# One core, one long list: the same 2118 entries handed to the scheduler in another order

## The chip, the core and the metric

The kernel runs on one core of a Trainium2 chip. The metric is the device time of one execution in microseconds (us); lower is better. The core has five engines that each work through their own instructions in program order: PE (TensorE, matmuls), DVE (VectorE), ACT (ScalarE), POOL (GpSimd) and SP (SyncE, which here only issues DMAs). They meet at semaphores: an instruction that needs another engine's result waits at the head of its own engine's queue, and everything behind it on that engine waits too.

## The reference: what is computed

There are two parts. The first is attention with a local window: 4 batches of 8 heads, 768 positions, 64 columns a head. Each position sees the positions less than 16 away, and 24 summaries of 32 positions each (the maximum of the keys, the mean of the values). The second is a network on the attention's result `x` (3072 rows of 512): `h = x @ w_in`, `g = h * cos(h)`, `out = g @ w_out`, with 2048 columns in the middle.

```python
mask_l = np.abs(pos[:, None] - pos[None, :]) < window
scores_s = scale * np.einsum('bhsd,bhnd->bhsn', q, k_sum) + np.log(block)
scores_all = np.concatenate([np.where(mask_l, scores_l, -1e9), scores_s], axis=-1)
a = np.exp(scores_all - np.max(scores_all, axis=-1, keepdims=True))
a = a / (np.sum(a, axis=-1, keepdims=True) + 1e-09)
x = np.matmul(a, np.concatenate([v, v_sum], axis=2))      # then heads side by side
h = x @ w_in
out = (h * np.cos(h)) @ w_out
```

## The kernel before

**Blocks, groups and steps.** The 3072 rows are cut into 8 blocks of 384 (two to a batch). In each block the attention of two heads is one *group*: a, b, c and d, so `c4` is the third group of block 4. The network of one block is 16 *steps*, one for each 128 of the 2048 middle columns. Steps are numbered through, s0 to s127: s0 to s5 do columns 0 to 5 of block 0 (their sums are put away), s6 to s21 all of block 1, s22 to s31 the rest of block 0, and from s32 on each block has 16 in a row. A step needs the `x` of all four groups of its block, in two parts (high and low). In its first product the groups are used in the order a, b, c, d, three matmuls each.

**Weights.** Each of the 16 weight slices w0 to w15 comes as 64-bit numbers and is turned by ACT, DVE (three passes of bit work) and POOL into a high and a low part. This is done once, between 11 and about 152 us, and works partly in PSUM banks and in the two "stage" tiles.

**The list.** The whole program is one list of entries, `ORDER`, read by the loop at the end. Each entry is `who.what.arguments`. The order of the entries of one engine is the order in which that engine runs them. Where two entries share a buffer, the one listed later waits for the one listed earlier. Numbers in `up`, `sc`, `ms`, `tq`, `tk`, `tp`, `va`, `dh` and `sh` are PSUM banks (there are 8); a last letter a, v or p is the engine (ACT, DVE, POOL).

The entries of a group, by engine: on SP `q`, `k`, `v`, `m` (loads; `m` takes the value summaries, from line 485), `po` and `pi` (out to DRAM and back, lines 640 and 647). On PE `tq` and `tk` (transposes), `ms` (the mask as a matmul), `sc` (scores, line 561), `tp` (transpose of the weights of the attention, line 618), `va` (values, line 662). On DVE `ks`, `mx` (maximum, line 580), `sm` (sum, line 601), `iv` (reciprocal, line 606), `qt`, `kt`, `pt` (transposes in squares of 32, lines 512, 517, 632) and `xl` (low part of x, line 348). On POOL `su` (less the maximum, line 585) and `nm` (normalize, line 609). On ACT `ex` (exp, line 598). `z` (line 572), `cp`, `cq`, `ck` and `xh` (line 342 on ACT, 344 on DVE) move results out of PSUM on the engine that their letter names.

So one group is a chain over all engines: `sc`, `z`, `mx`, `su`, `ex`, `sm`, `iv`, `nm`, then `tp` and `cp` (or, from group c2 on, `pt`, `po`, `pi`), `va`, `xh`, `xl`.

The entries of a step: `up` (PE, line 706: 12 matmuls into one bank), `tu` (ACT, line 716), `re` (DVE, line 719), `si` (ACT, line 724), `ga` (DVE, line 728; the bank is free after it), `hi` (ACT line 342 or DVE line 344), `lo` (DVE or POOL, line 348), `dh` and `dl` (PE, line 757: 6 and 3 matmuls into three banks of sums). `re` and `ga` of one step lie on DVE with `si` on ACT between them. After the last step of a block, `ta` and `st` take the sums out and store them.

A weight slice has `l` (load), `ab`, `cl`, `sh`, `lb`, `fb`, `hi`, `lo`; the value summaries `v0_1` and so on have `l`, `h` and `s`.

**Buffers that couple the engines.** The three tiles of a step (`t`, `gh`, `gl`) have two buffers each: a third `tu` waits for an earlier step's `lo`, a third `hi` for an earlier `dh`, a third `lo` for an earlier `dl`. The tile of loaded keys (`kn`) and that of loaded queries (`qn`) have one buffer from block 2 on.

## Time and profile before

| | us |
|---|---|
| median of 3 runs | 661.62 |
| lowest and highest of them | 660.22 and 662.21 |
| profiled execution, its own time | 663.55 |
| span in that execution, first to last instruction | 661.8 |
| PE busy | 633.2 |
| DVE busy | 449.9 |
| ACT busy | 305.8 |
| POOL busy | 220.7 |

The profile comes from one execution. A span is the time from the first to the last instruction. A group row gives the line, the engine and operation, output and inputs, the tile shapes, a count, the busy time, the mean ns of one, and the idle time of that engine before these instructions with what ended it.

### The profile page before, as it was taken

The page shows a single profiled execution, that of the slowest core. Times are in us where ns is not written, and L with a number is a line of the kernel's source. Part 1 is how long each engine was busy: PE and PEld are TensorE (multiplying, and loading weights), DVE is VectorE, ACT ScalarE, POOL GpSimd, SP SyncE. Part 2 cuts the span into 40 slices and gives each one's busy share as a digit, 9 for nine tenths or more (in the row PEclk, how much of TensorE's full clock was granted, in tenths as well). Part 3 has the DMA queues.
Part 4 walks back from the last instruction along what each step waited for, and adds up shares of the span by engine and source line. Part 5 has one row for each costly group of instructions (what it writes and reads, how often), then busy time and mean ns, then how long its engine had stood idle before and what let it go on. Part 6 is the DMA issues. An engine that isn't in the chain of part 4 may idle for free.

```text
span 661.8 us, 13155 instructions
## 1 busy us (share of the span) xinstructions
PE 633.2 (96%) x5141; PEld 560.9 (85%) x5141; DVE 449.9 (68%) x798; ACT 305.8 (46%) x512; POOL 220.7 (33%) x219
## 2 busy tenths in 40 slices
PE   6378999999999999999999999999999999999996
...
GB/s 222 257 271 188 289 16 215 173 113 63 59 125 82 93 120 122 139 58 113 109 104 137 137 96 106 116 43 85 108 169 101 93 94 76 0 1 17 16 17 48
DMA packets 167158, 72.67 MB, mean 110 GB/s; under 512 B 136825, under 2 KB 155833, under 8 KB 167097
## 3 DMA queue, kind: packets, MB, share of 16 engines
...
q8 instruction: 40, 0.66, 0.4%
...
## 4 chain that ended last, share of the span: by engine, by line
PE 86%; DMA 4%; SPq 3%; DVE 3%; POOL 2%; ACT 1%; issue 1%; DVEq 0%; POOLq 0%; ACTq 0%
PE banks L757 39%; PE banks L706 39%; PE banks L561 4%; PE banks L662 3%; DMA late<-in_moe_w_out_dram 2%; SPq L448 2%; DMA late<-in_moe_w_in_dram 1%; DMA late<-in_q_dram 1%; DVE banks L391 1%; DVE stage L407 1%; POOL stage L385 1%; ACT stage L380 1%; SPq L477 0%; PE banks L548 0%; DVE banks L399 0%
## 5 line engine op out<-in xcount | busy, mean ns | idle before, releaser
L706 PE MATMUL banks<-xh,w 128*128 128x384 f32 x1024 | 272.1, 337 | 0.2 <-ACT pt L342 0.2
L757 PE MATMUL banks<-w,gh 128*128 128x512 f32 x768 | 198.1, 393 | 0.0
L706 PEld LDWEIGHTS banks<-xh,w 128*128 128x128 f32 x1024 | 185.9, 188 | 2.9 <-ACT pt L342 0.4
L706 PE MATMUL banks<-xl,w 128*128 128x384 f32 x512 | 171.4, 335 | 0.0
L757 PEld LDWEIGHTS banks<-w,gh 128*128 128x128 f32 x768 | 142.6, 188 | 28.8 <-ACT gh L342 0.3
L716 ACT ACTIVATE t<-banks 128x384 int32<-128x384 f32 x128 | 62.5, 489 | 164.8 <-DVE gl L348 60.2
L348 POOL TENSOR_TENSOR gl<-t,gh 128x384 fp32r<-128x384 f32 x55 | 56.4, 1026 | 224.0 <-PE banks L757 108.3
L719 DVE SCALAR_TENSOR_TENSOR t<-t,banks 128x384 f32<-128x384 int32 x128 | 69.9, 548 | 67.3 <-ACT t L716 66.4
L757 PE MATMUL banks<-w,gl 128*128 128x512 f32 x384 | 109.8, 394 | 1.0 <-DVE gl L348 1.0
L724 ACT ACTIVATE t<-t 128x384 f32<-128x384 f32 x128 | 66.5, 524 | 75.5 <-DVE t L719 75.1
L706 PEld LDWEIGHTS banks<-xl,w 128*128 128x128 f32 x512 | 96.1, 188 | 1.6
L757 PEld LDWEIGHTS banks<-w,gl 128*128 128x128 f32 x384 | 71.1, 188 | 15.5 <-DVE gl L348 1.1
L585 POOL TENSOR_TENSOR sc<-sc,m 128x720 f32<-128x720 f32 x28 | 40.1, 1431 | 130.3 <-DVE m L580 130.3
L728 DVE TENSOR_TENSOR t<-t,banks 128x384 f32<-128x384 f32 x128 | 69.1, 544 | 13.4 <-ACT t L724 12.4
L609 POOL TENSOR_TENSOR sc<-sc,r 128x720 f32<-128x720 f32 x28 | 39.9, 1426 | 48.9 <-DVE r L606 45.6
L342 ACT CAST gh<-t 128x384 fp32r<-128x384 f32 x68 | 34.7, 511 | 43.9 <-DVE t L728 22.4
L348 DVE TENSOR_TENSOR gl<-t,gh 128x384 fp32r<-128x384 f32 x73 | 41.5, 569 | 18.0 <-PE banks L757 9.8
L344 DVE CAST gh<-t 128x384 fp32r<-128x384 f32 x60 | 23.1, 384 | 28.6 <-PE banks L757 26.8
L348 POOL TENSOR_TENSOR w<-stage,w 128x1024 fp32r<-128x1024 f32 x15 | 36.3, 2418 | 10.4 <-ACT w L342 8.5
L572 DVE SCALAR_TENSOR_TENSOR sc<-banks,mask 128x360 f32<-128x360 f32 x48 | 24.4, 524 | 21.2 <-PE banks L561 21.2
L561 PEld LDWEIGHTS banks<-kd,qd 64*64 64x64 f32 x1344 | 28.4, 135 | 9.2 <-issue 6.6
L662 PEld LDWEIGHTS banks<-pt,vn 120*64 120x64 f32 x624 | 21.0, 141 | 13.0 <-ACT pt L342 7.0
(101 smaller groups left out, 602.1 us busy)
## 6 DMA issues: line engine op xcount, KB each, us to landing
...
```

Of the source, the lines that this page charges most:

```text
L342: eng.copy(out=out, in_=in_)
L348: eng.tensor_tensor(out=lo, in0=src, in1=hi.bitcast(F32), op=ALU.subtract)
L561: nc.tensor.matmul(out=self.sp[hh][s * QT : (s + 1) * QT, c, lo : lo + n], lhsT=self.qd[rows, t * QT : (t + 1) * QT], rhs=self.kd[rows, ke ...
L585: nc.gpsimd.tensor_tensor(out=self.sc, in0=self.sc, in1=self.m.unsqueeze(2).broadcast_to([P, U, NK]), op=ALU.subtract)
L609: nc.gpsimd.tensor_tensor(out=self.sc, in0=self.sc, in1=self.r.unsqueeze(2).broadcast_to([P, U, NK]), op=ALU.mult)
L662: nc.tensor.matmul(out=self.xps[rows, t * QT : (t + 1) * QT], lhsT=self.vn[:, t, rows], rhs=self.pt[2 * c + hh][s], start=True, stop=True,)
L706: nc.tensor.matmul(out=self.h, lhsT=w_of(name, self.f)[:, c * P : (c + 1) * P], rhs=x_of(self.blk, part, c), start=n == 0, stop=n == last,)
L716: nc.scalar.activation(out=self.t.bitcast(I32), in_=self.h, func=AF.Copy, scale=1.0 / TWO_PI, bias=0.25)
L719: nc.vector.scalar_tensor_tensor(out=self.t, in0=self.t.bitcast(I32), scalar=-TWO_PI, in1=self.h, op0=ALU.mult, op1=ALU.add)
L724: nc.scalar.activation(out=self.t, in_=self.t, func=AF.Sin, scale=-1.0, bias=-0.5 * math.pi)
L728: nc.vector.tensor_tensor(out=self.t, in0=self.t, in1=self.h, op=ALU.mult)
L757: nc.tensor.matmul(out=self.acc[i], lhsT=g[:, i * P : (i + 1) * P], rhs=w_of(name, self.f), start=self.first and n == 0, stop=self.last an ...
```

## The change

`ORDER` is replaced by another list of the same 2118 entries: each entry of the old list is in the new one, on the same engine. What differs is the order on each engine and the PSUM banks in the arguments, which follow the order. No function, shape or buffer count changes. The diff is cut to the beginning, the end, and the places that the prediction speaks of.

```diff
--- before.py
+++ after.py
@@ -25,147 +25,147 @@
...
-b0.k a0.q a0.k c0.q c0.k b0.tk.0.0 d0.k b0.ks.0 a0.tq.1 b0.tk.1.2 v0_1.l b0.ks.1 a0.tk.0.3 a0.cq.v v0_0.l a0.tk.1.4
-b0.ck.0.v a0.ck.0.a a0.ks.0 a0.ms.5.6 a0.ck.1.a a0.ks.1 b0.q a0.sc c0.tk.0.7 a0.z.1.a a0.z.0.v w1.l c0.ck.0.a a0.mx
-d0.tk.0.1 c0.ks.0 a0.su c0.tq.0 c0.tk.1.3 d0.q c0.cq.a d0.tk.1.4 c0.ms.6.5 d0.ks.1 a0.ex v0_1.h.p c0.ks.1 c0.ck.1.v
-w0.l d0.ks.0 c0.sc a0.sm c0.v c0.z.1.a v0_0.h.v b0.tq.7 c0.z.0.a b0.ms.0.3 b0.ck.1.a a0.iv v0_0.s.p b0.cq.a v0_1.s.v
-d0.ck.0.a b0.sc w1.ab.0 c0.mx c0.m d0.tq.5 b0.z.1.a w1.cl.v c0.su d0.ms.2.1 b0.z.0.a w2.l w1.sh.6.7 d0.cq.a d0.ck.1.a
-d0.sc w1.lb a0.nm c0.ex a0.v d0.z.1.a w1.fb.1 a0.tp.0.3 d0.z.0.a a0.tp.1.0 w0.ab.0 a0.m d0.mx w1.hi.a w0.cl.v d0.su
-d0.m c0.sm w0.sh.4.5 w5.l w1.lo.p c0.iv w2.ab.0 w0.lb c1.m a0.cp.0.a w2.cl.v c0.nm d0.ex b1.q w0.fb.1 a0.cp.1.a w3.l
-a0.va.1 d0.sm w0.hi.a d1.m w2.sh.6.7 w0.lo.p c0.tp.0.2 c1.q d0.iv w5.ab.0 w2.lb b1.tq.3 a1.q a0.xh.a d0.nm c0.tp.1.0
-w2.fb.1 c0.cp.0.a d0.v c0.cp.1.a w5.cl.v w2.hi.a c0.va.2 a0.xl w2.lo.p d0.tp.0.6 c0.xh.a w5.sh.4.5 w4.l d0.tp.1.7 a1.m
-b0.mx w3.ab.0 a1.tq.0 w5.lb b0.su a1.v a1.cq.a a1.ms.1.0 w5.fb.1 w3.cl.p b0.ex b0.m d0.cp.0.a a1.sc b0.sm b1.cq.a
-c1.tq.6 d0.cp.1.a c0.xl a1.z.1.a d0.va.3 b0.iv w3.sh.4.5 b0.nm a1.z.0.a b1.m c1.ms.7.2 d0.xh.a a1.mx c1.cq.a d1.q
-w4.ab.0 c1.sc w3.lb a1.su b0.v b0.tp.0.0 w5.hi.a b0.tp.1.1 d0.xl w4.cl.v c1.z.0.a c1.v b0.cp.0.a w4.sh.6.7 c1.z.1.a
-b1.ms.3.0 b0.cp.1.a v1_0.l c1.mx a1.ex w8.l w4.lb c1.su b0.va.2 b1.sc a1.sm b0.xh.a w5.lo.p c1.ex d1.tq.1 b0.xl
-b1.z.1.a a2.q a1.iv s0.up.2 w4.fb.0 b1.z.0.a a1.nm w3.fb.1 w4.hi.a a1.tp.0.0 d1.cq.a w4.lo.v w9.l d1.ms.3.6 s0.tu
-a1.cp.0.a b1.v c1.sm w8.ab.0 a1.tp.1.7 d1.sc s0.re c1.iv a1.cp.1.a s1.up.4 w8.cl.v c1.nm w10.l s0.si b1.mx d1.v
-w8.sh.0.1 w3.hi.a b1.su a1.va.5 d1.z.0.v s1.tu c1.tp.0.7 w8.lb w3.lo.p a2.v d1.z.1.a c1.tp.1.3 a2.tq.6 s1.re c1.cp.1.a
-a1.xh.a s2.up.3 d1.mx s1.si c1.cp.0.a s0.ga d1.su w7.l w8.fb.0 s0.hi.a c1.va.2 s0.lo.p w9.ab.1 s1.ga w6.l s3.up.7
-w8.hi.v s2.tu b2.q s1.hi.v d1.ex w9.cl.v s1.lo.p a1.xl s0.dh.0.1.4 s2.re w8.lo.p c1.xh.v s3.tu s0.dl c1.xl s2.si s3.re
-s4.up.5 a2.cq.v v1_0.s.p d1.sm s3.si s2.ga s1.dh w7.ab.0 d1.iv s2.hi.v d1.nm v1_1.l w9.sh.2.3 s1.dl b1.ex s3.ga
-s2.lo.p d1.tp.0.6 w9.lb d1.tp.1.7 s2.dh w7.cl.p s4.tu b1.sm d1.cp.1.a s2.dl d1.cp.0.a s4.re b1.iv s3.hi.a d1.va.7
-w9.fb.1 b1.nm s4.si s5.up.6 w7.sh.2.3 s3.lo.p w9.hi.v d1.xh.a s3.dh s4.ga s5.tu w9.lo.p w10.ab.0 d1.xl s5.re s3.dl
-w7.lb s4.hi.a b1.tp.0.5 s5.si v1_1.s.p b1.tp.1.7 s4.dh b1.cp.1.a w7.fb.1 b1.cp.0.a s5.ga w7.hi.a b1.va.7 v1_2.l
-s4.lo.v w10.cl.v s4.dl s5.hi.a w7.lo.p b1.xh.a s5.dh b1.xl w10.sh.2.3 s6.up.5 v1_2.s.p w6.ab.1 w10.lb s7.up.6 w10.fb.0
-s6.tu s5.lo.p v1_3.l s6.re w12.l w6.cl.v s6.si s5.dl s7.tu w10.hi.v s8.up.7 s7.re w10.lo.p s5.ta.2.a s6.ga s7.si
-v1_3.s.v s9.up.2 s5.ta.1.a s7.ga v1_4.l s6.hi.a w6.sh.4.5 s5.st.2 s5.ta.0.a s6.lo.p b2.m s7.hi.a s10.up.3 s8.tu w6.lb
-s7.lo.p w12.ab.0 s8.re v1_4.s.p s11.up.6 w6.fb.1 s8.si s9.tu s8.ga v1_5.l w6.hi.a w12.cl.v s6.dh.4.5.7 w11.l s9.re
...
-s60.dh s62.re a5.su c4.xh.a b5.z.1.v a5.m s62.si s61.ga s63.up.2 b5.z.0.v s61.hi.a a5.v b5.mx a5.ex s61.lo.p c5.qt
-d4.va.7 b5.su s62.ga d5.q c4.xl s60.dl d4.xh.v b5.ex s61.dh s62.hi.v a5.sm s63.tu b5.m s61.dl d4.xl s63.re s64.up.3
-a5.iv s63.si b5.sm a5.nm s65.up.1 s62.lo.p a5.pt.0 v3_0.s.p s64.tu a5.po s64.re c5.sc.5.7 s63.ga s64.si v3_1.l s62.dh
...
-a7.q s86.lo.p c6.mx s88.tu d6.sc.4.6 s87.re c6.su b6.po a6.va.3 s87.si d6.z.1.v s79.st.2 s88.re s85.dl c6.m d6.z.0.v
-s88.si s89.up.6 s87.ga c6.ex a6.xh.v b6.v d6.mx s90.up.4 s87.hi.v d6.su c6.sm c6.v a6.xl d6.ex a7.qt s86.dh s87.lo.v
...
-s91.re s92.tu d6.m s91.si c6.va.4 a7.ex s89.dl s91.ga s92.re s90.dh b7.z.0.v c6.xh.v s91.hi.a s90.dl a7.sm d6.pi
...
-s126.hi.v s125.dl s126.lo.v s126.dh s127.ga s127.hi.a s126.dl s127.lo.p s127.dh s127.dl s127.ta.2.a s127.ta.0.0.v
-s127.st.2 s127.tb.2.v s127.st.0 s127.ta.1.1.v s127.sb.2 s127.st.1
+a0.k a0.tk.0.0 a0.ck.0.a a0.ms.1.2 a0.tk.1.3 a0.ck.1.a d0.k c0.k a0.q v0_1.l d0.q c0.q b0.q d0.tk.0.4 d0.ks.0 a0.ks.1
+a0.tq.5 a0.cq.v a0.ks.0 b0.k c0.tk.1.7 c0.tk.0.6 c0.ks.1 c0.ks.0 c0.ck.1.v d0.tk.1.3 a0.sc a0.z.1.a v0_1.h.p w1.l
+c0.tq.0 v0_0.l a0.z.0.v d0.ks.1 a0.mx c0.v c0.ms.5.7 c0.ck.0.a c0.cq.a a0.su a0.ex b0.tk.0.6 b0.tq.0 b0.cq.a b0.tk.1.2
+c0.sc c0.z.0.a d0.ck.0.a d0.tq.1 c0.z.1.a w1.ab.0 b0.ck.1.a d0.ck.1.a d0.ms.0.5 b0.ms.7.4 v0_1.s.v a0.sm b0.ks.1 c0.m
+b0.ck.0.v a0.iv b0.ks.0 a0.nm c0.mx c0.su b0.sc a0.tp.1.6 d0.cq.a d0.sc a0.tp.0.1 w0.l w1.cl.v b0.z.0.a c0.ex v0_0.h.v
+b0.z.1.a d0.z.1.a a0.cp.1.a d0.z.0.a w1.sh.2.3 a0.v b1.q c0.sm w1.lb d0.mx v0_0.s.p w2.l w1.fb.1 a0.m b0.mx w0.ab.0
+w0.cl.v w1.hi.a d0.su d0.ex w5.l w1.lo.p w0.sh.2.3 c0.iv w0.lb w0.fb.1 c0.nm c0.tp.0.0 a1.q d0.m w2.ab.0 b0.su d0.sm
+w0.hi.a w0.lo.p b1.tq.2 w3.l c0.tp.1.3 a0.cp.0.a a0.va.1 c1.q b1.cq.a b0.ex w2.cl.v d0.iv w2.sh.4.5 w2.lb w5.ab.0
+a1.ms.2.6 d0.nm a0.xh.a c0.cp.0.a c0.cp.1.a d0.v c0.va.0 w2.fb.1 w2.hi.a w2.lo.p w5.cl.v w5.sh.4.5 a0.xl w4.l
+d0.tp.1.3 c0.xh.a c0.xl w5.lb a1.tq.7 d0.cp.1.a d0.tp.0.1 a1.cq.a w3.ab.0 w3.cl.p b0.m b0.v b0.sm a1.sc a1.z.1.a
+c1.tq.0 c1.cq.a d0.cp.0.a c1.ms.3.7 a1.z.0.a w5.fb.1 b0.iv a1.mx d0.va.0 d0.xh.a c1.sc d1.q b0.nm d0.xl b1.ms.2.1
+w3.sh.4.5 c1.z.1.a c1.z.0.a c1.mx w4.ab.0 a1.su c1.su b0.tp.1.0 b0.tp.0.3 b0.cp.1.a b0.cp.0.a w3.lb b1.sc b0.va.0 a1.v
+c1.v w8.l w4.cl.v w4.sh.6.7 b1.z.0.a b0.xh.a b0.xl w4.lb v1_0.l b1.m a1.m w5.hi.a a1.ex a1.sm a1.iv c1.ex b1.z.1.a
+s0.up.3 d1.tq.0 s1.up.1 a1.nm w4.fb.0 w4.hi.a b1.mx c1.sm w5.lo.p a1.tp.1.2 d1.ms.6.7 s1.tu s0.tu a1.cp.1.a d1.cq.a
+w4.lo.v w7.l b1.su c1.iv c1.nm a2.q c1.m a1.tp.0.2 a1.cp.0.a w8.ab.0 d1.sc s2.up.0 w3.fb.1 d1.z.0.v s1.re w9.l w3.hi.a
+w3.lo.p v1_0.s.p v1_1.l c1.tp.0.2 w8.cl.v s0.re w8.sh.4.5 w8.lb a1.va.6 d1.z.1.a s4.up.7 s0.si s0.ga c1.cp.0.a s1.si
+s0.hi.a s0.lo.p a1.xh.a s1.ga d1.mx c1.tp.1.3 c1.cp.1.a s3.up.1 s1.hi.v w8.fb.0 d1.su b1.ex a1.xl a2.tq.2 c1.va.3
+s1.lo.p w8.hi.v w8.lo.p s0.dh.4.5.6 s0.dl s1.dh s1.dl c1.xh.v d1.ex s2.tu s2.re d1.sm s3.tu s2.si a2.cq.v d1.iv d1.nm
+w10.l d1.m d1.v w9.ab.1 s2.ga s3.re s2.hi.v s2.lo.p w7.ab.0 d1.tp.1.0 d1.tp.0.2 d1.cp.1.a s3.si s4.tu s2.dh s2.dl
+s5.up.0 v1_1.s.p b1.sm w9.cl.v c1.xl s3.ga b1.iv b1.nm d1.cp.0.a s4.re v1_2.l b1.v w6.l w9.sh.1.2 s3.hi.a s3.lo.p
+w7.cl.p b1.tp.1.3 s4.si s4.ga d1.va.7 s4.hi.a d1.xh.a s3.dh s3.dl w9.lb w9.fb.1 w9.hi.v b1.cp.1.a s5.tu s5.re d1.xl
+s4.lo.v w7.sh.1.2 b1.tp.0.3 s4.dh b1.cp.0.a b1.va.3 b1.xh.a w7.lb s4.dl b1.xl s6.up.7 s7.up.3 s5.si w10.ab.0 w9.lo.p
+w7.fb.1 w7.hi.a v1_2.s.p s5.ga w7.lo.p s6.tu s5.hi.a s5.lo.p w10.cl.v w10.sh.0.1 w10.lb w10.fb.0 v1_3.l w12.l b2.q
+s6.re v1_3.s.v w10.hi.v s6.si s6.ga w6.ab.1 w6.cl.v s7.tu s8.up.2 s5.dh s5.dl s5.ta.2.a s10.up.0 s7.re s7.si w6.sh.6.7
+s7.ga w6.lb s9.up.1 s11.up.3 w10.lo.p v1_4.l v1_4.s.p v1_5.l w12.ab.0 s6.hi.a s5.ta.0.a s5.st.0 s6.lo.p w6.fb.1 w11.l
+s7.hi.a s8.tu s5.ta.1.a s8.re w12.cl.v s7.lo.p s9.tu v1_5.s.p v1_6.l s9.re s9.si s9.ga s6.dh.4.7.6 s6.dl s8.si w6.hi.a
...
+c4.pi c4.va.2 b5.sc.4.6 c5.q s59.dh s61.up.7 a5.mx s59.lo.v s59.dl s62.tu s62.re s62.si c5.qt d4.m d4.po a5.v d4.pi
+d4.v d5.q s60.dh b5.z.1.v s60.lo.v a5.su a5.ex a5.sm a5.iv a5.nm a5.pt.0 s61.tu s61.re s61.si c4.xh.a s62.ga s62.hi.v
+s61.ga c4.xl b5.z.0.v b5.mx s61.hi.a s61.lo.p b5.su b5.ex b5.sm b5.iv s60.dl s63.up.6 s63.tu s63.re s63.si s63.ga
+s62.lo.p s61.dh s63.hi.v s61.dl s62.dh s62.dl d4.va.4 d4.xh.v c5.sc.1.2 d4.xl s64.up.6 s64.tu s64.re s64.si s63.lo.v
...
+b6.iv s84.dl s85.hi.v s85.lo.v s87.tu c6.z.0.v b6.nm s87.re b6.pt.0 c6.mx d6.qt a7.q s85.dh s89.up.5 s85.dl s86.lo.p
+s87.si s88.tu s87.ga c6.su s87.hi.v c6.ex s88.re s87.lo.v c6.sm c6.iv s86.dh s86.dl s87.dh s91.up.7 d6.kt.1 d6.ks.1
+s89.tu s89.re s89.si s88.si s89.ga s88.ga s88.hi.a d6.ks.0 a6.v a6.va.5 d6.sc.0.1 d6.z.1.v a7.qt s87.dl s89.hi.a
...
+s92.tu s91.lo.v b7.q b7.qt c6.m d6.v s79.st.2 c6.v s90.dh s93.up.2 s90.dl s91.dh s91.dl a7.z.0.v a7.mx s92.re d6.mx
+s92.si s92.ga b6.xh.a b6.xl d6.su a7.su d6.ex d6.sm d6.iv a7.ex a7.sm d6.nm s93.tu s92.hi.v a6.xl s93.re c6.pi c6.va.7
+b7.sc.0.1 a7.iv a7.nm d6.pt.1 b7.z.1.v b7.z.0.v b7.mx d6.po a7.m c7.q s94.up.5 s93.si s93.ga s92.lo.v s93.hi.a
+s93.lo.v s94.tu s94.re s94.si s94.ga s92.dh s94.hi.v b7.su a7.pt.0 b7.ex s95.up.0 s95.tu c7.qt s92.dl s94.lo.v s93.dh
+s93.dl s94.dh s94.dl c6.xh.v c6.xl s95.re s95.si s95.ga d6.m d6.pi c7.sc.5.7 d6.va.0 d6.xh.v d6.xl s102.up.2 b7.m
...
+s126.lo.v s127.tu s125.dl s126.dh s126.dl s127.re s127.si s127.ga s127.hi.a s127.dh s127.lo.p s127.dl s127.ta.2.a
+s127.ta.1.1.v s127.st.2 s127.st.1 s127.ta.0.0.v s127.tb.2.v s127.st.0 s127.sb.2
```

208 lines of the change are left out of this document (101 added, 107 removed).

## The prediction, as it was written before the result

> **What bounds the kernel now.** I read the page's slices first, then PE's waits, then windows by stage.
>
> ```profile
> PE   6378999999999999999999999999999999999996
> 20.00:40.00 20.00, 8.76 (x146) 6.60 (x140) 18.39 (x21) 12.11 (x20) 14.75 (x12) 0.76 0.87 253
> 60.00:80.00 20.00, 18.84 (x183) 16.31 (x182) 18.34 (x28) 16.61 (x27) 14.74 (x11) 1.00 1.00 300
> 80.00:100.00 20.00, 19.00 (x136) 16.00 (x135) 18.65 (x26) 13.35 (x21) 18.30 (x18) 1.00 0.15 40
> 98.00:657.00 559.00, 558.77 (x4305) 502.01 (x4303) 369.01 (x688) 245.79 (x415) 152.47 (x142) 1.00 0.35 92
> PE banks L757 <- DVE gl L348: 1.0, 1, 1.0
> ```
>
> The columns after the window are its length, then busy PE, PEld, DVE, ACT, POOL, then the granted clock. From 98 to 657 us PE is busy for 558.77 of 559 us at full clock: a new order can't shorten that stretch, only open holes in it. What can be won lies before 98. There PE is idle or waits, and DVE is busy 18.4 of 20 us from 20 to 40 and 18.65 from 80 to 100: DVE's list decides when PE fills up. PE's last wait, 1.0 us, is for DVE.
>
> The PE stream has these units, from the chain of waits and from PE's rows; they are the same instructions after the change:
>
> ```profile
> 151.34 2.09 PE banks L757 x9
> 188.40 2.10 PE banks L706 x12
> 198.81 1.02 PE banks L561 x36
> 199.82 0.85 PE banks L662 x24
> 59.51 0.44 PE L706 MATMUL banks<-xh,w 128*128 128x384 f32 x1
> 96.67 0.33 PE L706 MATMUL banks<-xh,w 128*128 128x384 f32 x1
> 109.89 0.39 PE L757 MATMUL banks<-w,gh 128*128 128x512 f32 x1
> 95.29 0.56 DVE L348 TENSOR_TENSOR xl<-banks,xh 128x384 fp32r<-128x384 f32 x1 [0.24 <-ACT xh L342]
> ```
>
> So an `up` is 2.09, `dh` 1.39, `dl` 0.70, `sc` 1.02, `va` 0.85. The last four rows are s0.up, s6.up, s6.dh and b1.xl, the last x that s6 needs: s6.up starts 0.8 us after b1.xl ends at 95.85.
>
> **The change, part by part.** The engine letters of all entries are the old ones, so no busy time is added or removed. I add up, along DVE's new order, what stands between an entry that PE releases and one that PE needs, with these prices:
>
> ```profile
> L719 DVE SCALAR_TENSOR_TENSOR t<-t,banks 128x384 f32<-128x384 int32 x128 | 69.9, 548 | 67.3 <-ACT t L716 66.4
> L728 DVE TENSOR_TENSOR t<-t,banks 128x384 f32<-128x384 f32 x128 | 69.1, 544 | 13.4 <-ACT t L724 12.4
> L724 ACT ACTIVATE t<-t 128x384 f32<-128x384 f32 x128 | 66.5, 524 | 75.5 <-DVE t L719 75.1
> L716 ACT ACTIVATE t<-banks 128x384 int32<-128x384 f32 x128 | 62.5, 489 | 164.8 <-DVE gl L348 60.2 <-PE banks L706 58.1 <-POOL gl L348 45.7
> L344 DVE CAST gh<-t 128x384 fp32r<-128x384 f32 x60 | 23.1, 384 | 28.6 <-PE banks L757 26.8
> L348 DVE TENSOR_TENSOR gl<-t,gh 128x384 fp32r<-128x384 f32 x73 | 41.5, 569 | 18.0 <-PE banks L757 9.8 <-ACT gh L342 7.1
> L348 DVE TENSOR_TENSOR xl<-banks,xh 128x384 fp32r<-128x384 f32 x32 | 17.5, 546 | 1.4 <-ACT xh L342 1.2
> L344 DVE CAST xh<-banks 128x384 fp32r<-128x384 f32 x13 | 7.2, 554 | 9.7 <-PE banks L662 9.5
> L572 DVE SCALAR_TENSOR_TENSOR sc<-banks,mask 128x360 f32<-128x360 f32 x48 | 24.4, 524 | 21.2 <-PE banks L561 21.2
> L580 DVE TENSOR_REDUCE m<-sc 128x6 f32<-128x720 f32 x28 | 24.9, 891 | 1.5 <-ACT sc L342 1.2
> L601 DVE TENSOR_REDUCE r<-sc 128x6 f32<-128x726 f32 x28 | 25.2, 899 | 7.6 <-ACT sc L598 7.4
> L606 DVE RECIPROCAL r<-r 128x6 f32<-128x6 f32 x32 | 5.8, 182 | 0.3
> L632 DVE STREAM_TRANSPOSE stage<-sc 128x768 f32<-128x768 f32 x22 | 21.3, 969 | 8.7 <-POOL sc L609 8.6
> L585 POOL TENSOR_TENSOR sc<-sc,m 128x720 f32<-128x720 f32 x28 | 40.1, 1431 | 130.3 <-DVE m L580 130.3
> L598 ACT ACTIVATE sc<-sc 128x720 f32<-128x720 f32 x28 | 22.6, 808 | 7.0 <-POOL sc L585 6.8
> L598 ACT ACT_TABLE_LOAD x22 | 28.2, 1283 | 0.4
> L399 DVE SCALAR_TENSOR_TENSOR banks<-late,banks 128x1024 int32<-128x1024 int32 x16 | 19.6, 1223 | 0.2
> L391 DVE TENSOR_SCALAR banks<-stage 128x1024 int32<-128x1024 int32 x16 | 19.5, 1221 | 1.7 <-POOL stage L385 0.9 <-ACT late L342 0.6
> L407 DVE SCALAR_TENSOR_TENSOR stage<-late,banks 128x1024 int32<-128x1024 int32 x16 | 19.4, 1212 | 2.6 <-POOL w L348 2.2
> ```
>
> DVE also waits inside its own order, where too little stands between two entries of a chain through another engine. From `mx` to `sm` lie `su` 1.43, `ex` 0.81, some 0.2 for hand-overs, and a table load in 22 of 32 cases (1.28 x 22/32 = 0.9, taken as 1.0): 3.44. From `iv` to `pt` lie 1.43 + 0.15 = 1.58, from `re` to `ga` 0.52 + 0.16 = 0.68. The hand-overs are estimates. I tried the sum on the old list: 6.0 us of such waits before `sm` (measured 7.4, row L601), 8.0 before `pt` (8.6, L632), 9.0 before `ga` (12.4, L728), and no PE hole beyond 0.03 us after s6, where PE has none. On the new list it gives 13.8 before `sm`, 4.4 before `pt`, 31.3 before `ga`, since chains stand close together (`b5.mx` is followed on DVE by `b5.sm` itself; in the old list eleven entries stand between).
>
> *The beginning (0 to 120 us): gain 0.9.* DVE's work up to b1.xl falls from 81.7 to 79.1 us, because less of the w slices and of block 1's `tu` to `lo` stands ahead of it. With the same idle time b1.xl ends 2.6 earlier, at 93.25. From there it costs: the new list has s7 two `up`s before s5.dh, and s11.up (bank 3) needs s7.ga. DVE has 12.9 us between b1.xl and s7.ga's end (w10, w6 and a value summary are in it), PE 12.0: 1.0 lost. Going on to s14.up, which needs s11.ga, 0.7 more. So 2.6 - 1.7 = 0.9. Both lists have the same 77.5 us of PE work up to s11.up's end, so this moves the total. Bounds: DVE's idle time before b1.xl is 95.85 - 81.7 = 14.1 us now. Following the new list load by load I get 12, the least, so 3.0 gained at best. At worst the new SP order adds 2.5: `v0_0.l` is now behind `w1.l`, and `c0.m`, which waits for DVE's `v0_1.s`, now stands ahead of `w0.l`, so w0, w2 and everything behind them on SP's queue waits too. That is a loss of 1.6.
>
> *The middle (120 to 600 us): loss 5.1.* Three of the nine places where the new order comes out short:
> - From b5.sc's end to the part of s64.up that reads d4's x, PE has two `up`s, four `dh`, four `dl`, a `va`, a `sc`: 14.4, and the first nine matmuls of s64.up, 1.5: 15.9. DVE has, from b5.z.1 to d4.xl, 19 entries worth 10.8 (2 z, lo, 2 sm, 2 iv, pt, 2 re, 3 ga, 2 hi, 2 xl, xh, mx) and waits of 0.66 (a5.sm), 1.58 (a5.pt), 3.44 (b5.sm), 0.68 (s63.ga): 17.2, 17.3 with hand-overs. Short by 1.4. Behind the waiting a5.sm stand s61.re and s61.ga, for which PE waits at s61.dh.
> - From s84.dh's end, which frees s85.hi's buffer, to d6.sc PE has 11.3; DVE from s85.hi to d6.ks.0 19 entries, 10.9, and waits 0.83 (c6.sm) and 0.68 (s89.ga): 12.4. With hand-overs, short by 1.3.
> - From s92.up's end to d6.va (bank 0, needs s95.ga) PE has 19.5; DVE from s92.re 27 entries, 16.5, waits 3.8 (2.35 of them d6.sm), and 0.7 for s92.tu ahead of it: short by 1.6.
> - The other six, in the same way: 0.44 (d2.sc), 0.12 (s32.up), 1.1 (a5.sc), 0.4 (s68.dh), 0.34 (b7.va), 0.41 (s126.up).
>
> The sum is 7.1. Where all exps find their table in place it is 3.1. I take the middle, 5.1, since both cases occur. Bounds: at least 1 (if DVE's real work runs ahead as in the old list, where the same sum is short nowhere), at most 9 (PE holes from ACT's and SP's order added).
>
> The Trainium skill (ScalarE: Activation LUTs, "What ACT_TABLE_LOAD costs") gives about 2.66 us for a switch of tables, a load of 1283 ns and a drain of 1380. The row of table loads above has 22 of 1283 ns with 0.4 us of idle time before them in all, so the trace agrees with the load and has no such drain. By the page's figure the four `sm` waits above would each be 1.38 longer and the loss of the middle 5.1 + 5.5 = 10.6; the sum goes by the row.
>
> *The end: nothing.* The last three `ta` and four stores stand in another order behind the same last `dl`.
>
> ```profile
> 657.56 0.68 DVE L795 TENSOR_SCALAR stage<-banks 128x512 f32<-128x512 f32 x1
> 658.61 0.40 SPq L813 DMA_DIRECT2D out_dram<-stage  x1
> ```
>
> DVE's work behind the last `dl` is the same three entries, and SP issues four stores in either order: within 0.2 us.
>
> *Loads of the middle.* In the new list some value loads stand just ahead of their `va` (`d7.v`, `d7.m`), but on SP's queue their buffer is free long before: 18 us of PE work or more lie between the `va` that frees it and the `va` that needs it. No cost; without that cover about 4 us a group.
>
> **The sum.** 661.8 - 0.9 + 5.1 = 666.0 for the span. The profiled execution took 663.55 with its span of 661.8; the median of the runs is 661.62, so 4.2 more is **665.8**.
>
> **The rivals.**
> - *The beginning wins (faster).* b0's chain comes early (b0.mx stands 12.8 us of DVE work sooner), so s0.up starts near 55 instead of 59.5 and DVE idles 12 us instead of 14.1 before b1.xl. For: the load sum, 79.1 to 81.7. Against: the 1.7 us lost again by s14. It decides if s6.up starts before 92.3 and the middle costs 1 or less: -3.0 + 1.0 gives 659.6, and 659.0 with a middle of 0.4.
> - *Gain and loss cancel.* Beginning -2.5, middle 3.1: 662.2. For: half of the middle's loss hangs on table loads.
> - *The start's loads come late.* SP's queue waits at `c0.m`, w0 lands after w1 has left DVE, then `w2.l` waits for `v0_0.s` on POOL. Beginning +1.6, middle 7.1: 670.3. For: DMA share 0.87 and 1.00 in two of the windows above. Against: as many loads stand ahead of w1 as before.
>
> **How the numbers follow.** A difference under 0.3% (2 us) can't be told from none here. Forecast (663.6 to 669) 0.47, late start (above 669) 0.11: slower 0.58. Cancelling 0.24. Beginning wins 0.18. The range reaches from 659.5, the faster rival, to 670.5, the late start's time; the forecast's own is 663.6 to 669.
>
> **What would show it.** Right: PE busy under 558 of any 559 us after 100, with waits at L706, L561 or L662 for DVE; idle before L601 near 14 us and before L728 near 30; s6.up at 93 to 95; PE busy again 633. Wrong: PE without holes after 100 (then my middle is wrong), or s6.up before 92 (then the beginning is). A single PE wait above 2 us after 120 us would be something I have not seen.

## The result, and the profile after

The median after the change is 666.61 us (666.23 to 668.39), beside 661.62 before (660.22 to 662.80): ratio 1.0085, with a 95% interval of 1.0062 to 1.0108. So the new order is slower by 5.0 us between the medians, 4.1 to 7.1 by the interval. The forecast was 665.8, and slower.

The profiled execution took 666.61 with a span of 664.8, so it stands at its median; the one before stood 1.9 above its own. That is why the two traces differ by only 3.0 in their spans.

From the page of the kernel after, the busy times and PE's slices:

```profile
PE 633.1 (95%) x5141; PEld 558.6 (84%) x5141; DVE 464.0 (70%) x798; ACT 301.9 (45%) x510; POOL 222.0 (33%) x219
PE   6479999999999999999999999999999999999996
```

PE's work is the old 633. DVE's busy time is not: 449.9 before, 464.0 now, with the same 798 instructions. The windows of the kernel after (length, then busy PE, PEld, DVE, ACT, POOL, clock):

```profile
98.00:657.00 559.00, 554.03 (x4263) 494.93 (x4262) 377.87 (x683) 243.00 (x412) 150.03 (x136) 1.00 0.35 90
...
320.00:530.00 210.00, 206.56 (x1772) 183.48 (x1771) 149.73 (x274) 91.61 (x150) 50.76 (x45) 1.00 0.39 100
...
120.00:320.00 200.00, 200.00 (x1636) 179.21 (x1635) 145.70 (x263) 94.84 (x154) 69.17 (x65) 1.00 0.44 109
530.00:650.00 120.00, 120.00 (x724) 108.09 (x724) 57.79 (x112) 40.16 (x79) 14.80 (x13) 1.00 0.13 39
```

In the 559 us in which PE idled 0.23 before, it now idles 4.97: 3.44 between 320 and 530, none in the windows on either side of it. The rest is one wait of 1.5 at s11.up, at 104. PE's waits from 300 to 650 us (total, times, longest):

```profile
PE banks L757 <- DVE gh L344: 1.3, 2, 1.0
PE banks L561 <- DVE xl L348: 0.6, 1, 0.6
PE banks L662 <- DVE t L728: 0.5, 1, 0.5
PE banks L662 <- DMA pd<-stage: 0.5, 1, 0.5
PE banks L706 <- DVE t L728: 0.3, 1, 0.3
PE banks L662 <- DMA vn<-in_v_dram: 0.2, 1, 0.2
```

By time these are s56.dh (0.29 at 333), a5.sc (0.64 at 339), b5.va (0.19 at 391), s76.up (0.28 at 418), s85.dh (0.98 at 474), a6.va (0.51 at 485) and d6.va (0.53 at 518). The one put down to the DMA is a6.va. It writes bank 5, which s89.ga on DVE frees at 484.58, and starts at 484.63: DVE again. The groups of the kernel after that answer to those shown of before:

```profile
L728 DVE TENSOR_TENSOR t<-t,banks 128x384 f32<-128x384 f32 x128 | 69.0, 547 | 34.9 <-ACT t L724 34.0
L348 DVE TENSOR_TENSOR gl<-t,gh 128x384 fp32r<-128x384 f32 x73 | 45.3, 626 | 15.3 <-PE banks L757 7.5 <-ACT gh L342 6.7
L344 DVE CAST gh<-t 128x384 fp32r<-128x384 f32 x60 | 26.2, 439 | 13.9 <-PE banks L757 10.6 <-DVE t L728 0.5
L601 DVE TENSOR_REDUCE r<-sc 128x6 f32<-128x726 f32 x28 | 25.2, 901 | 12.5 <-ACT sc L598 12.5
L632 DVE STREAM_TRANSPOSE stage<-sc 128x768 f32<-128x768 f32 x22 | 21.3, 968 | 7.2 <-POOL sc L609 4.6 <-DMA out_dram<-stage 2.6
L348 DVE TENSOR_TENSOR xl<-banks,xh 128x384 fp32r<-128x384 f32 x32 | 17.4, 548 | 2.1 <-ACT xh L342 1.9
L385 DVE TENSOR_SCALAR stage<-stage 128x1024 f32<-128x1024 f32 x14 | 14.6, 1046 | 0.2 <-ACT stage L380 0.2
...
L598 ACT ACT_TABLE_LOAD x21 | 26.9, 1283 | 0.4
```

The row of L385 in the kernel before, for comparison:

```profile
L385 DVE TENSOR_SCALAR stage<-stage 128x1024 f32<-128x1024 f32 x14 | 11.4, 818 | 3.5 <-ACT stage L380 3.4
```

The waits in DVE's order grew as forecast: ahead of L728 from 13.4 to 34.9, ahead of L601 from 7.6 to 12.5. What wasn't forecast is in the means. `gl` went from 569 to 626 ns, `gh` from 384 to 439, while `xl` (548), which is the same subtraction but reads a PSUM bank, and L728, which reads one too, kept theirs.

**How the kernels are compared below.** Executions of one kernel differ by 2 to 4 us, mostly by what happens before 60 us (by then the PE work done in six profiles of the same new beginning is already 1.9 us apart). So beside the times I use PE's *lead*: the PE entries that have started by a moment, each weighted with its steady length (`up` 2.05, `dh` 1.44, `dl` 0.66, `sc` 1.18, `va` 0.96, fitted to stretches without holes), less the same sum in the profile of before. A fall of the lead is time lost at that place. In the kernel after it is 5.3 at 95 us, 3.2 at 130, 3.2 at 320, -2.4 at 530 and -3.0 at the end: 2.1 lost around 105 and 6.2 from 320 on. That is more than the 3.44 of holes that the windows show. A matmul's record lasts 335 to 395 ns where its successor starts 173 to 227 ns later, so of each wait the first 0.15 or so shows as busy; for seven waits that is some 1.1 of the 2.8, and 0.6 falls behind 530, where PE shows no wait. The rest stays unexplained. The leads are taken against a profile that stood 1.9 above its median, so a lead of 0 at the end is not a tie with the median.

### The profile page after: what moved, and what is told of

It is laid out like the page before. It is cut to its first block, busy times and chain, and to the rows that moved or that the text cites. A ratio compares the mean times of both kernels' runs of the same rounds, so it can differ in the third digit from the quotient of the medians.

```text
span 664.8 us, 13139 instructions
## 1 busy us (share of the span) xinstructions
PE 633.1 (95%) x5141; PEld 558.6 (84%) x5141; DVE 464.0 (70%) x798; ACT 301.9 (45%) x510; POOL 222.0 (33%) x219
## 4 chain that ended last, share of the span: by engine, by line
PE 74%; DVE 6%; SPq 1%; ACT 1%; issue 1%; DMA 1%; POOL 0%; DVEq 0%; ACTq 0%; POOLq 0%
PE banks L706 34%; PE banks L757 34%; PE banks L561 3%; PE banks L662 3%; DVE gl L348 1%; DVE t L719 1%; DVE t L728 1%; DVE stage L632 1%; DMA vn<-in_v_dram 1%; DVE m L580 1%; DVE gh L344 0%; ACT t L716 0%; POOL sc L585 0%; ACT t L724 0%; DVE stage L385 0%
## 5 line engine op out<-in xcount | busy, mean ns | idle before, releaser
L706 PE MATMUL banks<-xh,w 128*128 128x384 f32 x1024 | 278.1, 338 | 1.8 <-DVE t L728 1.8
L348 POOL TENSOR_TENSOR gl<-t,gh 128x384 fp32r<-128x384 f32 x55 | 56.8, 1039 | 200.9 <-PE banks L757 92.3
L728 DVE TENSOR_TENSOR t<-t,banks 128x384 f32<-128x384 f32 x128 | 69.0, 547 | 34.9 <-ACT t L724 34.0
L348 DVE TENSOR_TENSOR gl<-t,gh 128x384 fp32r<-128x384 f32 x73 | 45.3, 626 | 15.3 <-PE banks L757 7.5
L348 POOL TENSOR_TENSOR w<-stage,w 128x1024 fp32r<-128x1024 f32 x15 | 36.8, 2451 | 17.4 <-ACT w L342 9.1
L344 DVE CAST gh<-t 128x384 fp32r<-128x384 f32 x60 | 26.2, 439 | 13.9 <-PE banks L757 10.6
L601 DVE TENSOR_REDUCE r<-sc 128x6 f32<-128x726 f32 x28 | 25.2, 901 | 12.5 <-ACT sc L598 12.5
L561 PE MATMUL banks<-kd,qd 64*64 64x24 f32 (+1 forms) x1344 | 31.0, 231 | 0.7 <-DVE xl L348 0.6
```

What stands on the lines that cost most here:

```text
L344: eng.tensor_copy(out=out, in_=in_)
L348: eng.tensor_tensor(out=lo, in0=src, in1=hi.bitcast(F32), op=ALU.subtract)
L561: nc.tensor.matmul(out=self.sp[hh][s * QT : (s + 1) * QT, c, lo : lo + n], lhsT=self.qd[rows, t * QT : (t + 1) * QT], rhs=self.kd[rows, ke ...
L706: nc.tensor.matmul(out=self.h, lhsT=w_of(name, self.f)[:, c * P : (c + 1) * P], rhs=x_of(self.blk, part, c), start=n == 0, stop=n == last,)
L728: nc.vector.tensor_tensor(out=self.t, in0=self.t, in1=self.h, op=ALU.mult)
```

## The experiments

All edit `ORDER` alone; the code blocks name long pieces of a list in words and cut others with dots. Ratios are to the kernel before, timed on the same chip at the same time.

| run | median | ratio (95%) | lead at 95, 130, 320, 530 us, end |
|---|---|---|---|
| the change | 666.61 | 1.0085 (1.0062 to 1.0108) | 5.3, 3.2, 3.2, -2.4, -3.0 |
| new until 95 us, then old | 664.63 | 1.0045 (1.0028 to 1.0063) | 4.4, -0.4, -0.4, -0.4, -0.4 |
| new until 210, then old | 663.40 | 1.0018 (1.0003 to 1.0032) | 4.7, 2.5, 1.3, 1.2, 1.2 |
| old until 210, then new | 675.12 | 1.0194 (1.0172 to 1.0215) | 1.2, 1.2, -6.2, -10.2, -11.1 |
| out of POOL's way | 665.72 | 1.0056 (1.0037 to 1.0074) | 3.6, 1.4, 1.3, -1.1, -1.7 |
| waits in DVE's order | 666.11 | 1.0054 (1.0037 to 1.0071) | 4.0, 1.8, 1.8, -0.9, -1.5 |
| w10.hi later | 669.32 | 1.0098 (1.0069 to 1.0127) | 4.5, 1.2, 0.9, -3.0, -3.6 |
| old, w9.hi later | 663.72 | 1.0011 (0.9996 to 1.0026) | 0.8, 0.6, 0.7, 0.6, 0.6 |
| all three sets of moves | 664.98 | 1.0039 (1.0021 to 1.0057) | 5.0, 1.7, 1.7, 0.6, 0.0 |
| new until 125, then old | 668.94 | 1.0103 (1.0083 to 1.0122) | 4.1, 1.9, -4.5, -4.4, -4.6 |
| the same, w10 and w12 later | 668.95 | 1.0099 (1.0082 to 1.0117) | 4.0, 2.0, -4.9, -4.9, -5.1 |
| old until 170, then new | 668.88 | 1.0104 (1.0079 to 1.0128) | 1.8, 1.8, 1.6, -3.7, -4.3 |
| new until 210, clean seam | 662.44 | 0.9996 (0.9981 to 1.0010) | 3.1, 0.9, 0.4, 0.4, 0.4 |

**Which part of the list does what.** Two lists can be joined where they have done nearly the same entries.

```diff
-ORDER = the whole new list
+ORDER = the first 363 entries of the new list + the old list without them
```

> The first 363 entries of the new list (to about 95 us), then the old list's order for the rest; one bank number differs. In the profiles the new list is 5.2 us of PE work ahead at 95 us, 3.3 ahead from 115 to 330 us, and 3.0 behind at the end. Theory (the two effects add, and each belongs to its part of the list): the lead of 5.2 comes from the entries before 95 us, and the old rest neither has the 1.5 us wait at s11.up nor a hole after 120 us, so 4 to 5 us of the lead stay: 656.6 to 657.7. Rival (the lead is only borrowed from the old order's own work and DVE gives it back before 150 us whatever follows): 660 to 661.6, no different from before.

Neither held. The lead of 4.4 at 95 us was gone by 105. At 95 the new list is ahead on PE partly because it has put off DVE's work. b1.xl ends 4.6 earlier than before, but w7.fb, s5.ga and w10.cl, 2.5 us, stand behind it and not ahead of it, and then w6.cl takes 2.61 for 0.90: s7.ga comes 1.0 earlier, not 4.6. My seam made it worse: s8.up shares bank 7 with s6.up, and PE's longest wait from 90 us on is that one:

```profile
PE banks L706 <- DVE t L728: 2.4, 1, 2.4
```

At its end PE's granted clock goes to 0.50, from 100.2 to 103.6 us, which costs PE up to 1.7 more (half of 3.4). So a lead in PE work is worth something only where the other engines' work is equal too.

```diff
-ORDER = the whole new list
+ORDER = the first 839 entries of the new list + the old list without them
```

> The first 839 entries of the new list (to about 210 us), then the old order; 27 entries have other bank numbers. Theory: the new list's lead of 3.1 at 210 us stays to the end, since the old order has no PE hole behind it: 658.5 (657.8 to 659.3). Rival (the holes after 330 us are the consequence of what the new beginning leaves behind, not of the later order): 664 to 667.

The time, 663.40, meets neither range. But the old order behind the new beginning has no hole after 260 us: the lead stays at 1.2, so the holes are not what the new beginning leaves behind. At the seam, c3.sc waits 0.7 for a bank that s31.ad.0 frees, and 1.2 of lead went there:

```profile
PE banks L561 <- DVE stage L774: 0.7, 1, 0.7
```

```diff
-ORDER = the whole new list
+ORDER = the first 839 entries of the old list + the new list without them
```

> The mirror of the run before: the first 839 entries of the old list, then the new order; 22 entries have other bank numbers. Theory: no lead, and the 6.1 us that the new list loses between 210 us and the end: 667.7 (666.5 to 668.5). Rival (the holes belong to what the new beginning leaves behind): 661.6.

The time can't be read for the question: the seam alone (c3.sc 1.7 and a3.va 2.0 of waits between 239 and 244, and the lead falls from 1.3 to -5.0) cost 6. The waits are only 3.8 of it. From 242.5 us on PE's granted clock also stands at 0.50 for 6.8 us (windows of this run: length, busy PE, clock):

```profile
236.00:242.00 6.00, 4.11 (x62) 1.00 0.23 82
242.50:249.30 6.80, 5.42 (x33) 0.50 0.75 195
```

From 260 us on -5.0 becomes -11.1, 6.0 lost, but not in the same places as in the change. Some 1.1 go at s52.up, which waits at 312 for s51.ga because the two share bank 2 in this run alone. From 320 on the loss is 4.9, and s85.dh's hole is missing. The mirror was made again at a place without a seam's wait:

```diff
-ORDER = the whole new list
+ORDER = the first 711 entries of the old list + the new list without them, its banks renamed throughout
```

> The mirror, with a clean seam: the first 711 entries of the old list (to about 170 us), then the new order with its bank numbers renamed. This shows what the new middle alone costs. Theory (the holes behind 320 us belong to the new order and not to what precedes it): 5.8 to 6.3 us as in the profile of the new list, ratio 1.0085 to 1.0095. Rival (the new middle is only that slow with the new beginning ahead of it): ratio 1.000 to 1.004.

The lead is still 1.6 at 320 and falls to -4.3: 5.9 there, with holes at five of the change's seven entries, of the same length within 0.02. The windows and the waits after 100 us:

```profile
320.00:530.00 210.00, 206.94 (x1774) 183.54 (x1773) 150.16 (x275) 91.76 (x150) 51.67 (x45) 1.00 0.39 100
```

```profile
PE banks L757 <- DVE gh L344: 1.3, 2, 1.0
PE banks L561 <- DVE xl L348: 0.6, 1, 0.6
PE banks L662 <- DVE t L728: 0.5, 1, 0.5
PE banks L662 <- DMA pd<-stage: 0.5, 1, 0.5
```

The ratio, 1.0104 (1.0079 to 1.0128), is 6.9 us, and the range given lies inside its interval. So the new middle costs about 6 with either beginning, and the rival falls.

**What makes the holes.** Around the largest, the timelines of DVE, POOL and PE in the kernel after (start, length, instruction, idle before it and what ended it):

```profile
472.13 0.18 DVE L606 RECIPROCAL r<-r 128x6 f32<-128x6 f32 x1
472.48 1.59 DVE L344 CAST gh<-t 128x384 fp32r<-128x384 f32 x1 [0.16 <-PE banks L757]
474.10 1.25 DVE L348 TENSOR_TENSOR gl<-t,gh 128x384 fp32r<-128x384 f32 x1
```

```profile
472.46 1.39 POOL L609 TENSOR_TENSOR sc<-sc,r 128x720 f32<-128x720 f32 x1 [3.51 <-DVE r L606]
473.81 1.12 POOL L348 TENSOR_TENSOR gl<-t,gh 128x384 fp32r<-128x384 f32 x1
```

```profile
472.28 0.86 PE L757 MATMUL banks<-w,gl 128*128 128x512 f32 x3
474.12 1.66 PE L757 MATMUL banks<-w,gh 128*128 128x512 f32 x6 [0.98 <-DVE gh L344]
```

b6.iv releases b6.nm on POOL. The next DVE instruction, s85.hi, a cast of 0.36 elsewhere, starts 20 ns behind it and ends only after it. s85.dh waits for that cast. Two sets of moves tell this apart from the waits inside DVE's order:

```diff
-... s86.hi.a b6.iv s84.dl s85.hi.v s85.lo.v s87.tu ...
+... s86.hi.a s85.hi.v s85.lo.v b6.iv s84.dl s87.tu ...
-... d5.sm d5.iv ... s69.lo.v s69.dh ...
+... d5.sm s69.lo.v d5.iv ... s69.dh ...
...
```

> The new list with seven DVE entries moved by a few places (s55.lo, s56.hi, s56.lo, s69.lo, s85.hi and s85.lo, s92.hi, s92.lo), and the order of the other engines left alone. In the profile of the new list these copies and subtractions ran while POOL worked on the scores, and took 0.7 to 1.6 us instead of 0.36 and 0.55. Theory (DVE's work on SBUF alone is held up by POOL, and that is what opens the holes at s56.dh, 0.29, and s85.dh, 0.98, and part of a5.sc's 0.64): each moved entry takes its 0.36 or 0.55, these holes close, and the time falls by 1.3 to 2.2 from the new list's 666.6: 664.4 to 665.3. Rival (the waits inside the chains mx to sm and iv to pt make the holes, as the prediction had it, and the long copies only fill time in which DVE would wait): 666 to 667, with the holes still there or a few places further on.

(The entries listed there are eight.) The moved cast is short again and PE runs on; the timelines of DVE and PE in this run:

```profile
473.16 0.36 DVE L344 CAST gh<-t 128x384 fp32r<-128x384 f32 x1 [0.24 <-PE banks L757]
473.55 0.56 DVE L348 TENSOR_TENSOR gl<-t,gh 128x384 fp32r<-128x384 f32 x1
474.03 0.18 DVE L606 RECIPROCAL r<-r 128x6 f32<-128x6 f32 x1
```

```profile
472.96 0.86 PE L757 MATMUL banks<-w,gl 128*128 128x512 f32 x3
473.65 1.58 PE L757 MATMUL banks<-w,gh 128*128 128x512 f32 x6
```

The holes at s56.dh and s85.dh are gone, a5.sc's 0.64 stayed. The loss from 320 us on is 3.0 in place of 6.2, and the ratio 1.0056 in place of 1.0085, 1.9 us; by the intervals that could be anything from about 0 to 3.9, so the size rests on the lead. Seven of the eight came out at their short price; s92.hi ran into a7.su at its new place (0.91). Together the eight took 4.4 us in place of 9.8. The waits inside DVE's order stayed what they were (34.4 ahead of L728 for 34.9, 13.2 ahead of L601 for 12.5, 7.0 ahead of L632 for 7.2), so it isn't through them that the moves work.

```diff
-... d4.iv c4.pt.0 a4.xl ...
+... d4.iv a4.xl c4.pt.0 ...
-... s73.lo.v c5.xh.v s74.si s74.ga ...
+... s73.lo.v s74.si s74.ga c5.xh.v ...
-... d6.kt.1 d6.ks.1 s89.tu s89.re s89.si ...
+... s89.tu s89.re d6.kt.1 d6.ks.1 s89.si ...
-... c6.xh.v c6.xl s95.re s95.si ...
+... s95.re c6.xh.v c6.xl s95.si ...
```

> The new list with five DVE entries moved so that PE is not behind a wait inside DVE's order: a4.xl ahead of c4.pt, s89.re ahead of d6.kt and d6.ks, s74.ga ahead of c5.xh, s95.re ahead of c6.xh. No entry is moved out of POOL's way. The holes in the profile of the new list that this aims at are a5.sc 0.64, a6.va 0.51, s76.up 0.28 and d6.va 0.53, 1.96 in all. Theory (two causes beside each other, waits in DVE's order and DVE held up by POOL): these four close, those at s56.dh (0.29) and s85.dh (0.98) stay, and the time is 664.4 to 665.2 where the new list takes 666.6 (0.2 to 0.3% less; about 1.0055 of the kernel before). Rival (DVE held up by POOL is the whole cause, and the four holes only show where DVE's lateness surfaces): the holes move on to the next entries, and the time stays within 0.5 of 666.6.

(The entries listed there are four.) The four holes aimed at closed (a6.va to 0.2), the ratio fell to 1.0054, as the theory gave it, and the loss from 320 on to 3.3. At s89.ga and s95.ga, on which a6.va and d6.va wait, DVE had stood idle 0.59 behind `re`; with two entries moved into that place it stands idle 0.00. That is the prediction's mechanism. The other two moves put an entry ahead of work that waits for nothing. But s85.dh's hole closed as well, which I had said would stay. The timelines of DVE and POOL in this run show why:

```profile
472.58 0.36 DVE L344 CAST gh<-t 128x384 fp32r<-128x384 f32 x1
472.98 1.63 DVE L348 TENSOR_TENSOR gl<-t,gh 128x384 fp32r<-128x384 f32 x1
```

```profile
472.58 1.60 POOL L609 TENSOR_TENSOR sc<-sc,r 128x720 f32<-128x720 f32 x1 [3.51 <-DVE r L606]
```

Here both start at 472.58; now the cast takes its 0.36 and POOL's instruction is the longer one (1.60 for 1.39), and s85.lo behind it pays (1.63). A few ns decide which of the two is held up. In the five profiles that have this pair unaltered, the cast starts 19 and 22 ns behind POOL's instruction and takes 1.59 and 1.58 (the change, old until 170), or 2, 4 and 13 ns ahead of it and takes 0.36, with POOL's at 1.60 (this run, w10.hi later, old until 210). From 320 on the first two lose 6.2 and 5.9; of the others, the two whose list is unaltered from there on lose 4.5 and 4.9. So some 1.2 of the 2.9 that this run takes off the loss is that accident, and some 1.7 is the moved entries: the prediction's cause is real, and smaller than POOL's part.

```diff
 all moves of the two runs above, and
-... s6.re v1_3.s.v w10.hi.v s6.si ... s7.ga w6.lb ...
+... s6.re v1_3.s.v s6.si ... s7.ga w10.hi.v w6.lb ...
```

> The new list with the moves of the POOL run (seven entries out of POOL's way after 320 us), of the chain run (five entries) and of the beginning (w10.hi) together. If the three add: 666.6 - 1.9 (measured for the first) - 2.0 - 1.3 = 661.4, ratio to the kernel before about 1.000, and in the profile no hole above 0.3 us after s7. If they overlap (the same lateness of DVE counted twice): 663 to 664.5, ratio 1.002 to 1.004.

The ratio, 1.0039, lies in the range for overlap. s6.dh and s8.dh wait 2.0 and 0.7, as in the run with w10.hi alone below. The windows of this run show 0.09 of idle time of PE between 320 and 530:

```profile
320.00:530.00 210.00, 209.91 (x1796) 187.62 (x1796) 147.50 (x280) 94.44 (x155) 50.84 (x45) 1.00 0.40 101
```

The loss from 320 us on is 1.7 where each set alone left 3.0 and 3.3, so of 6.2 the first takes 3.2, the second 2.9, both 4.5. They overlap by 1.6, of which s85.dh's hole, closed in each, is 1.2. The last 1.7 I have not explained; 0.6 of it falls between 530 and 640, where PE shows no wait.

**The beginning.** The third set, alone:

```diff
-... s6.re v1_3.s.v w10.hi.v s6.si ... s7.ga w6.lb ...
+... s6.re v1_3.s.v s6.si ... s7.ga w10.hi.v w6.lb ...
```

> The new list with one DVE entry moved: w10.hi behind s7.ga. In the profile of the new list w10.hi releases w10.lo on POOL (2.4 us), and the next DVE entry, w6.cl, takes 2.64 us instead of 0.69; s7.ga, for which s11.up waits 1.52 us, stands behind it. Theory (DVE held up by POOL matters in the beginning too): w6.cl takes 0.7, s11.up waits for nothing, and 1.0 to 1.5 us of lead are added: 665.1 to 665.6. Rival (DVE is the bound there whatever the order, so the entry that is put off is missed at s14.up or s18.up): 666.2 to 667.

What it aimed at, from the timelines of DVE and POOL in the kernel after:

```profile
99.31 2.64 DVE L385 TENSOR_SCALAR stage<-stage 128x1024 f32<-128x1024 f32 x1
```

```profile
99.01 2.39 POOL L348 TENSOR_TENSOR w<-stage,w 128x1024 fp32r<-128x1024 f32 x1 [2.99 <-DVE w L344]
```

w6.cl did fall to 0.68 and s11.up's wait went (and in the middle, which is untouched, s85.hi came first as above, and the loss from 320 on is 4.5). But s6.dh then waited 2.0 and s8.dh 0.7, and the kernel got no faster (1.0098, 1.0069 to 1.0127, beside the change's 1.0085). On ACT w12.ab waits for the buffer that w10.lo frees, and s6.hi stands behind it. ACT's timeline in that run:

```profile
105.39 1.12 ACT L380 ACTIVATE stage<-late 128x1024 f32<-128x1024 f32 x1 [4.15 <-POOL w L348]
106.42 0.49 ACT L342 CAST gh<-t 128x384 fp32r<-128x384 f32 x1
```

The same in the old list, for w9.hi, which took 1.71 beside POOL there:

```diff
-... s3.lo.p w9.hi.v d1.xh.a s3.dh s4.ga s5.tu w9.lo.p w10.ab.0 d1.xl s5.re ...
+... s3.lo.p d1.xh.a s3.dh s4.ga s5.tu d1.xl s5.re w9.hi.v w9.lo.p w10.ab.0 ...
```

> The old list with one DVE entry moved: w9.hi behind s5.re, with w9.lo behind it. In the profile of before w9.hi took 1.71 us instead of 0.69, because b1.nm and s3.lo ran on POOL, and s4.ga, d1.xl and in the end b1.xl, for which s6.up waits, stand behind it. Theory: w9.hi takes 0.7, s6.up starts about 1.0 earlier, and the time is 0.5 to 1.0 below the kernel before (ratio 0.9985 to 0.9992). Rival (w9.lo and what follows on POOL come later and hold up DVE again): no change (1.000).

w9.hi took 0.69; s4.dl then waited 1.5 for s4.lo where it had waited 1.0, and no change of the time can be told (0.9996 to 1.0026).

What is the new beginning worth by itself? The run with the new list until 210 us spoke to that; here the join is earlier:

```diff
-ORDER = the whole new list
+ORDER = the first 485 entries of the new list + the old list without them, its banks renamed throughout
```

> The first 485 entries of the new list (to about 125 us), then the old order with its bank numbers renamed throughout, so that no entry at the seam waits for a bank. This shows what the new beginning alone is worth. Theory (the prediction's terms, a gain of about 1 in the beginning and all of the loss behind it; the 3.3 us of lead in the first pair of profiles is partly the spread between executions): 660.8 to 661.8, ratio 0.9975 to 0.999. Rival (the beginning is worth the full 3.3): 659.1, ratio 0.995. Rival (the beginning is worth nothing, its lead being taken back by DVE before 125 us): ratio 1.000.

No entry is out of place in the list, yet s15.up waited 4.9 for a bank that a weight slice's last pass frees:

```profile
PE banks L706 <- DVE stage L407: 4.9, 1, 4.9
```

The lead fell from 1.9 to -4.6 at the seam (here too the clock reads 0.50 at the end of the wait, from 135.3 to 138.7), so the time tells nothing of the beginning, and none of the three ranges was met. The next had the same seam:

```diff
 as the run before, and
-... s6.re v1_3.s.v w10.hi.v s6.si ... s7.ga w6.lb ... w10.lo.p v1_4.l v1_4.s.p v1_5.l w12.ab.0 s6.hi.a ...
+... s6.re v1_3.s.v s6.si ... s7.ga w10.hi.v w6.lb ... s6.hi.a ... s7.lo.p w10.lo.p ... s9.ga w12.ab.0 ...
```

> As the run before, and in the beginning w10.hi stands behind s7.ga on DVE, w10.lo behind s7.lo on POOL, and w12.ab behind s9.si on ACT, so that neither w6.cl runs beside w10.lo nor s6.hi stands behind w12.ab, which waits for w10.lo's buffer. Theory (the earlier run with w10.hi alone failed because of w12.ab on ACT's queue): w6.cl takes 0.7, s11.up and s6.dh wait for nothing, 1.0 to 2.0 us less than the run before. Rival (DVE is full there, and what is put off is missed at s14.up): the same time as the run before, or up to 1 more.

Beside the run before: s11.up and s6.dh wait for nothing, the lead at 110 us is 3.6 in place of 2.4, and at 130 it is 2.0 in place of 1.9. What is won is missed at s8.dh (1.3, for s8.hi on ACT). The rival had that right, but named DVE and s14.up; and with the long wait of s15.up behind it, the time (668.95 for 668.94) could not have shown a gain. (w12.cl on DVE, which needs w12.ab, moved with it.)

```diff
 as the run with the new list until 210 us, and
-... s37.tu s37.re s31.ad.0 s37.si ...
+... s31.ad.0 s37.tu s37.re s37.si ...
```

> The run with the new list until 210 us and the old order behind it, with one DVE entry moved: s31.ad.0 ahead of s37.re. In that run c3.sc waited 0.7 us for a bank that s31.ad.0 frees, and the lead in PE work fell from 2.4 to 1.2 us there, at the seam. With the seam closed the lead of the new beginning should stay to the end. Theory (the new beginning is worth about 1 us, as the prediction had it, and the rest of the first pair's lead is spread between executions): 661.0 to 662.2 beside a kernel before of 662.2, ratio 0.998 to 1.000. Rival (it is worth the 3.3 us of the first pair of profiles): ratio 0.995 to 0.996. Rival (it is worth nothing): 1.000 to 1.002, and the same as the run without this move.

c3.sc's wait is gone, PE has no wait behind the 1.5 at s11.up, which ends at 106, and the ratio is 0.9996 (0.9981 to 1.0010). 0.5 of the lead still went at the seam. That rules out a beginning worth 3.3, and can't tell one worth 1 from one worth nothing. This is the fastest of the kernels made and no faster than the one before that can be measured.

## Why the prediction was right

Time, sign and size came out: 665.8 for 666.61, +4.2 for +5.0. The bound was read rightly, and the loss lies in the middle, as forecast. But the two sizes behind the sum, 0.9 and 5.1, came near by errors that cancelled; that part is luck. Step by step:

- **What bounds it: right.** PE busy 633.1, no single wait above 2 us (the longest after 60 us is 1.5).
- **"No busy time is added or removed": wrong.** DVE's rose by 14.2 us: the durations summed by 10.6 (4.2 in `gl`, 3.3 in `gh`, 3.2 in L385, small differences both ways elsewhere), and the rest because the records of neighbours overlap by 0.08 where none waits, which is rarer now. I priced `gh` and `gl` at the means of their rows and took a mean for a constant. The trace of before already held casts of 0.54, 0.82 and 1.26 among its 60.
- **The beginning, gain 0.9: not contradicted, its first term near by luck.** In the six executions with the new beginning unaltered (the change, the two sets of moves, and the three joins at 125 and 210 us) b1.xl ends at 90.3 to 92.6, mean 91.6; in the three with the old one at 94.0 to 95.8, mean 94.8. That is 3.2 earlier for 2.6.
  - The step behind it failed: I let DVE's work fall by 2.6 at the same idle time. DVE's busy time up to b1.xl's end falls by 0.6 only (mean 77.2 for 77.8), its idle time by 2.7 (14.3 for 17.0). The three entries that the new list puts off (w7.fb, s5.ga, w10.cl) are worth 2.5, as I had it, but in the first pair of profiles the rest takes 1.9 more than before, w4.lo, v0_0.h and s2.hi above all. A shorter idle time was what my first rival had; no run shows where it comes from. My list prices were 4.0 too high on the old side (81.7 for 77.7) and 2.0 on the new (79.1 for 77.1).
  - The lead falls by 2.1 or 2.2 between 95 and 130 in each of the six, for 1.7. The wait at s11.up in it goes when POOL doesn't hold up w6.cl, so that part isn't the listed work either.
  - What is left at 130 is 0.9 to 3.2, mean 2.0, against 0 to 1.8, mean 1.0: 1.0 for 0.9, from so few and so spread executions that it can't be told from nothing. The first pair of profiles shows 3.2, above my bound of 3.0, because one was the quickest of the new and the other the slowest of the old.
  - I had said that s6.up before 92 would prove this step wrong. It started at 89.83, and between 90.5 and 92.1 in the other five. The test forgot the spread of the starts, but the step with the idle time was indeed wrong.
- **The middle, loss 5.1: near in size (6.2 and 5.9, or 4.9 and 4.5 where s85.hi came first), for the smaller part right in its cause.** The waits that I added up are there in total (34.9 ahead of L728 for 31.3, 12.5 ahead of L601 for 13.8, 4.6 for POOL ahead of L632 for 4.4), and moving four entries takes some 1.7 off. The larger part, 3.2 (1.2 of it at s85.dh), is DVE's copies held up by POOL, a term that my sum lacked. Of the nine places, a hole came at two (a5.sc, forecast 1.1, where the lead falls by 1.4 with s56.dh's; d6.va, forecast 1.6, 0.6) and near two more (s68.dh, forecast 0.4: b5.va, 0.5; d6.sc, forecast 1.3: s85.dh and a6.va, 2.3 together). Nothing came at d2.sc, s32.up, s64.up, b7.va and s126.up, and s76.up was not on my list. The sum of nine came out closer than the nine.
- **The table loads: the price right, its place in the sum wrong.** 21 loads of 1283 ns come before exps, with 0.4 of idle time in all. But I added 1.0 for a load to every wait from `mx` to `sm`. Where `sm` stands right behind `mx`, at b5, the load is over before `su` starts, and DVE waits 2.41, not 3.44; at d6 it runs while `su` does. The timelines of ACT, POOL and DVE in the kernel after:

```profile
358.83 1.28 ACT L598 ACT_TABLE_LOAD   x1
361.62 0.81 ACT L598 ACTIVATE sc<-sc 128x720 f32<-128x720 f32 x1 [1.51 <-POOL sc L585]
```

```profile
360.19 1.39 POOL L585 TENSOR_TENSOR sc<-sc,m 128x720 f32<-128x720 f32 x1 [0.23 <-DVE m L580]
```

```profile
362.46 0.91 DVE L601 TENSOR_REDUCE r<-sc 128x6 f32<-128x726 f32 x1 [2.41 <-ACT sc L598]
```

The other three waits at `sm` came out at 0.47 (a5, for 0.66), 0 (c6, for 0.83) and 1.48 (d6, for 2.35), while those without a load fit: 1.57 for 1.58 at a5.pt, 0.63 for 0.68 at s63.ga, 0.59 for 0.68 at s89.ga. With the measured waits s64.up, short by 1.4 in my sum, is short by 0.1, and no hole came there. My own sum without loads was 3.1; the 2.0 that I put on top for them stood in for the 3.2 of POOL, which was luck. The drain that the Trainium skill adds (ScalarE: Activation LUTs, "What ACT_TABLE_LOAD costs") would have given 10.6 for the middle; it does not show.
- **The end, nothing: right.** From PE's last matmul to the end of the span 5.0 before and 5.0 after.
- **Loads of the middle, nothing: right for PE but for b5.va's 0.2.** DVE waits 3.5 for a6's keys at 422, and PE has no wait for the next 50 us.
- **The rivals.** "The beginning wins" fell by the middle, as its own condition said. The late start didn't come: s0.up starts earlier in every execution (53.7 to 55.9 for 58.0 to 59.5).
